# The second part of a 2-D spectral filter: 64x64 fp32 products on quarters of the TensorE array instead of split 128x128 products

## The chip, the cores and the metric

The kernel runs on one core of a Trainium2 chip. A core has a matrix engine (TensorE, PE in the profile), a vector engine (VectorE, DVE), a scalar engine for functions such as exp (ScalarE, ACT), GpSimd (POOL) and a synchronising engine that issues transfers (SP). TensorE reads its operands from SBUF and writes its results to PSUM, which has eight banks of 128 partitions x 2 KB. One bank holds one 128x512 fp32 result. The metric is the device time of one execution, in microseconds (us); the number of a kernel is the median over its runs.

## What is computed

Two independent results stand side by side in the output. The first is multi-query attention: 16 heads share one key and one value of width 28. The second is a global filter: a real 2-D FFT of a 2048 x 448 array, a product with a complex weight for each frequency, and the inverse FFT.

```python
# A: x (1, 2048, 448), 16 heads of 28, one k and one v
q = (x @ wq) as (1, 16, 2048, 28);  k = x @ wk;  v = x @ wv
scores = einsum("bhqd,bkd->bhqk", q, k) * 28 ** -0.5
a = (softmax(scores) @ v, heads side by side) @ wo
# B: x (1, 2048, 448), w_r and w_i (2048, 225)
X = rfft2(x) * (w_r + 1j * w_i)
b = irfft2(X, s=(2048, 448))
out = concatenate([a, b], axis=-1)
```

## The kernel before

**Attention.** Four heads are packed into one group, and there are four groups (g) for each of four chunks of 512 queries (c). Each of these 16 pairs (c, g) has 16 steps, one for each block of 128 keys. A step makes four score tiles of 128x512 (L914, one matmul each, the operands split so that single-pass fp32r products keep fp32 accuracy), takes their exponentials (L846 straight from PSUM on ScalarE), and multiplies them by the values (L857: four fp32 matmuls of 128 rows x 32 columns that run side by side in the four column strips of the array; an fp32 matmul is two passes, so the trace shows eight records). The sums of the 16 steps gather in one PSUM bank.

**Rounds.** Steps are done in rounds. In a round of six steps all 24 score tiles are made first, then the value products of six steps. Some tiles are "lazy": VectorE copies the scores to SBUF (L920) and ScalarE takes their exponentials later, during the value products (L939 or L943). The table `PLAN` lists the rounds as strings: `-` is a score tile whose exponential is taken at once, `k` a lazy tile, `e` a tile of a late step whose exponential ScalarE takes from PSUM (L925), and capital letters are units of other work put between the score tiles. The program itself is written out in that order; each engine executes its own instructions strictly in it.

**Banks.** A score tile or a unit takes a bank with `take()`, and the reader of the result gives it back with `give()`. Which bank is taken is fixed when the program is built, from a model of when each will be free (`clock`, `passed`, `at_once`). One bank holds the running sums of the value products, so seven banks rotate among score tiles and units. VectorE work that can wait is put into a queue (`put`), from which the planner lets it out where its model has VectorE idle; `need` forces it out before an instruction that depends on it.

**The filter.** It has three parts. The first (`fft1`) ends at about 73 us, before the rounds start in earnest. The third (`fft3`, letter Z) has its first matmul at 308.8 us and runs almost to the end. The second part is the one that changes. It works on 16 slices u of two columns each (2 x 225 = 450 frequencies), all 128 partitions. A forward unit (letter A, `fft2_a`) multiplies the slice by a fixed 128x128 matrix g1 (32-point transforms, real and imaginary parts), then VectorE multiplies by the complex weights. A backward unit (letter B, `fft2_b`) multiplies by g2, VectorE copies the result to SBUF (L636), and every second unit a transfer takes it to the DRAM array t2. Both matrix products go through `mm3`: matrix and data are split into a high and a low fp32r half, and three 128x128 products are added up (L567, L568, L569). The splits of the data cost VectorE a cast and a subtraction before each product (L598 and L599 for the forward one, L621 and L622 for the backward one). The complex product is L612 and L613 (each 64 partitions, crossing the halves), L614, and later L620.

The second part lies in 17 rounds between 86.0 and 302.7 us: one round with A alone, eleven with B and A, four with B, A and X (X is four W units, the 11 matmuls of the output projection of one block, L767), and a round of five steps with B alone.

Of the kernel before, what the change touches and what calls it, by code (L numbers as in the profile page):

```python
# [48 lines left out]
PLAN += [spread(6, "A", 6, 1.6, 0.85, 1.5)] + 11 * [spread(6, "BA", 6, 0.9, 0.6, 1.5)]  # L49
PLAN += 4 * [spread(6, "BAX", 5, 0.9, 0.85, 1.5)] + [spread(5, "B")] + [spread(7, "ZZ", 8, 0.9, 0.85, 2.0)]  # L50
# [16 lines left out]
def kernel(ctx: ExitStack, tc: tile.TileContext, t: dict):  # L67
# [120 lines left out]
    def fft2_consts():  # L188
        for n in ("g1", "g2"):
            g = fp.tile([128, 128], F32, name=n, tag="g", bufs=1)  # L190
            nc.gpsimd.dma_start(g, t[n])
            h = fc[n + "h"] = fp.tile([128, 128], F32R, name=n + "h", bufs=1)
            l = fc[n + "l"] = fp.tile([128, 128], F32R, name=n + "l", bufs=1)
            nc.gpsimd.tensor_copy(h, g)
            nc.gpsimd.tensor_tensor(l, g, h.bitcast(F32), op=ALU.subtract)
# [370 lines left out]
    def mm3(out, w, h, l):  # L566
        mm(out, fc[w + "h"], h, start=True, stop=False)  # L567
        mm(out, fc[w + "l"], h, start=False, stop=False)  # L568
        mm(out, fc[w + "h"], l, start=False, stop=True)  # L569
# [5 lines left out]
    def fft2_load(q):  # L575
        b = b2["b", q] = fp.tile([128, 4, DF], F32R, name="b2", tag="b2")
        for r in range(2):
            for l in range(2):
                p = (r * 2 + l) * 32
                ld = nc.sync.dma_start(b[p:p + 32].bitcast(F32), t1v[r, l][:, 4 * q:4 * q + 4])  # L580
# [12 lines left out]
    def fft2_split(u):  # L593
        q, v = divmod(u, 2)
        b = b2["b", q][:, 2 * v:2 * v + 2]
        bh = b2["h", u] = fp.tile([128, 2, DF], F32R, name="bh", bufs=1)
        put(("split", u), [
            (400, lambda: nc.vector.tensor_copy(bh, b.bitcast(F32))),  # L598
            (630, lambda: nc.vector.tensor_tensor(b, b.bitcast(F32), bh.bitcast(F32), op=ALU.subtract))], True)  # L599

    def fft2_a(u):
        q, v = divmod(u, 2)
        s = slice(2 * v, 2 * v + 2)
        b, wr, wi = (b2[n, q][:, s] for n in ("b", "wr", "wi"))
        need(("split", u))
        need(("pr", u - 1))
        bank = take()
        pu = halves2(bank)
        mm3(pu, "g1", b2["h", u], b)
        passed(608)  # L610
        pf, p2 = fp.tile([128, 2, DF], F32, name="pwr"), fp.tile([128, 2, DF], F32, name="pwi")
        nc.vector.tensor_tensor(p2[0:64], pu[64:128], wi[64:128], op=ALU.mult)  # L612
        nc.vector.tensor_tensor(p2[64:128], pu[0:64], wi[0:64], op=ALU.mult)  # L613
        nc.vector.tensor_tensor(pf, pu, wr, op=ALU.mult)  # L614
        at_once(1800)
        give(bank)
        h = fp.tile([128, 2, DF], F32R, name="ph")
        p = fp.tile([128, 2, DF], F32R, name="pl")
        put(("pr", u), [
            (700, lambda: nc.vector.scalar_tensor_tensor(pf, p2, sgn, pf, op0=ALU.mult, op1=ALU.add)),  # L620
            (420, lambda: nc.vector.tensor_copy(h, pf)),  # L621
            (640, lambda: nc.vector.tensor_tensor(p, pf, h.bitcast(F32), op=ALU.subtract))], True)  # L622
        if u < 15:
            fft2_split(u + 1)
        pr[u] = h, p

    def fft2_b(u):
        v = u % 2
        need(("pr", u))
        bank = take()  # L630
        pc = halves2(bank)
        mm3(pc, "g2", *pr.pop(u))
        passed(608)
        if v == 0:
            cst[0] = fp.tile([128, 4, DF], F32, name="cst")
        nc.vector.tensor_copy(cst[0][:, 2 * v:2 * v + 2], pc)  # L636
        at_once(600)
        give(bank)
        if v:
            nc.sync.dma_start(t2[:, 2 * u - 2:2 * u + 2], cst[0])  # L640


    def fft3_consts():
        c = fp.tile([113, 4, 113], F32, name="cs3", tag="wi")
        behind(nc.gpsimd.dma_start(c, t["cs3"]), begun[-1])
        h = fc["cs3h"] = fp.tile([113, 4, 113], F32R, name="cs3h", tag="cs", bufs=1)
        l = fc["cs3l"] = fp.tile([113, 4, 113], F32R, name="cs3l", tag="bh", bufs=1)
# [3 lines left out]
    t2v = t2.rearrange("(r l n) h f -> r l h n f", r=2, l=2)  # L651
    c2 = {}

    def fft3_load(q):
        c2["c", q] = fp.tile([128, 4, DF], F32, name="c2", tag="b2")
        for r in range(2):
            for l in range(2):
                p = (r * 2 + l) * 32

                eng = nc.gpsimd if q == 0 and r else nc.sync  # L660
                eng.dma_start(c2["c", q][p:p + 32], t2v[r, l][:, 4 * q:4 * q + 4])
# [136 lines left out]
    def at(step, f, *a):  # L798
# [3 lines left out]
            "A": [(fft2_a, u) for u in range(16)],  # L802
            "B": [(fft2_b, u) for u in range(16)],
# [14 lines left out]
    at(where["A"][0] - 1, fft2_split, 0)  # L818
    at(where["B"][-1] + 1, fft3_consts)
    for u, step in enumerate(where["A"]):  # L820
        if u % 2 == 0 and u < 14:
            at(step - 1, fft2_load, u // 2 + 1)
    for g in range(2 * NG - 1):
        at(where["B"][g + 1] - 4, wo_load, g)
        at(where["B"][g + 1] + 4, wo_split, g)
    for q in range(8):
        at(max(where["Z"][4 * q] - 8, where["Z"][4 * q - 5] + 1 if q > 1 else where["B"][-1] + 1), fft3_load, q)
# [42 lines left out]
    def after(step):  # L870
# [5 lines left out]
        if step == where["B"][-1] + 1:  # L876
            spans.extend(fp.tile([128, 2, CW], F32, name="p", tag="wr") for _ in range(2))
# [190 lines left out]
def _constants():  # L1068
# [13 lines left out]
    c["sgn"] = np.where(np.arange(128) < 64, -1.0, 1.0)[:, None]  # L1082
# [29 lines left out]
    def blocks(sign):  # L1112
        a, b = np.cos(sign * a32), np.sin(sign * a32)
        e = np.eye(2)
        return np.block([[np.kron(e, a), np.kron(e, b)], [-np.kron(e, b), np.kron(e, a)]])
# [5 lines left out]
def _layout(A_x, A_wq, A_wk, A_wv, A_wo, B_x, B_w_r, B_w_i):  # L1121
# [24 lines left out]
    for n, w in (("wr", B_w_r), ("wi", B_w_i)):  # L1146
        z[n] = np.asarray(w)[:, order].reshape(32, 32, 2, DF).transpose(2, 0, 1, 3).reshape(64, 32, DF)
# [36 lines left out]
```

## Time and profile before

| What | Value |
|---|---|
| median of 3 runs | 636.54 us (636.4 to 636.67) |
| the profiled execution | 636.34 us, of which the span is 634.6 us |
| TensorE busy (its ends are modelled) | 628.0 us, 99% |
| ScalarE busy | 547.4 us, 86% |
| VectorE busy | 450.7 us, 71% |
| GpSimd busy | 61.0 us, 10% |
| granted TensorE clock | 1.0 (full) throughout |

The span runs from the first to the last instruction of the program. A busy TensorE row does not mean that TensorE works at its peak: records of matmuls overlap and their ends are modelled. More is told by the distance from one matmul's start to the next one's, and by the idle time that the profile prints behind a weight load (PEld) with the instruction that ended it. In timelines the columns are the start, the length, the engine, the line, the operation, output and inputs, the shape, and how many equal instructions were merged into the row.

### The profile page before, as it was taken

The numbers are of one execution on the slowest core, as the hardware profiler recorded it, in microseconds if no ns is written. First come the engines' busy times: TensorE is split into PE (matmuls) and PEld (weight loads), VectorE is DVE, ScalarE is ACT, GpSimd is POOL, SyncE is SP. The second block draws the span as 40 slices with busy tenths as digits, with TensorE's granted clock in tenths as the row PEclk, the third lists the DMA queues.
The fourth block names the chain that finished last, engine by engine and source line by source line (L and its number), as shares of the span: only waits on it lengthen the run. The fifth ranks groups of instructions, "written<-read, shape, count | busy, mean of one in ns | idle before, by whom it ended". The sixth has DMA issues, their size and how long they took to land. (4 is left out here: it accounts for less than half of the span.)

```text
span 634.6 us, 12172 instructions
## 1 busy us (share of the span) xinstructions
PE 628.0 (99%) x4442; PEld 378.3 (60%) x4442; DVE 450.7 (71%) x808; ACT 547.4 (86%) x987; POOL 61.0 (10%) x118
## 2 busy tenths in 40 slices
PE   8999999999999999999999999999999999999997
PEld 6877655665565466664555665565556565555555
DVE  5999648989998977676766755277777764467653
ACT  5554999999999998888989998999989989989991
POOL 3021401010321020000110100001010100000000
PEclk9999999999999999999999999999999999999999
DMA  8755972645543734133342403034322322030011
GB/s 272 274 156 159 264 186 52 164 122 143 160 96 98 184 80 123 58 81 129 101 101 56 115 15 82 15 84 145 79 68 76 89 82 74 16 82 14 17 31 61
DMA packets 37315, 66.74 MB, mean 105 GB/s; under 512 B 7945, under 2 KB 21786, under 8 KB 36284
## 3 DMA queue, kind: packets, MB, share of 16 engines
q1 hardware_dynamic: 32032, 52.50, 29.9%
q0 software_dynamic: 4640, 12.48, 7.4%
q8 instruction: 36, 0.59, 0.4%
q10 hardware_dynamic: 576, 0.92, 0.4%
q14 instruction: 31, 0.25, 0.1%
HBM read 29.81 MB, written 17.87 MB: 75 GB/s over the span
## 5 line engine op out<-in xcount | busy, mean ns | idle before, releaser
L846 ACT ACTIVATE p<-s 128x512 f32<-128x512 f32 x425 | 234.7, 645 | 25.0 <-PE s L914 24.5
L914 PE MATMUL s<-qa,ka 128*128 128x512 f32 x779 | 235.0, 404 | 0.0
L914 PEld LDWEIGHTS s<-qa,ka 128*128 128x128 f32 x779 | 142.1, 188 | 63.6 <-issue 27.7
L920 DVE COPY k<-s 128x512 f32<-128x512 f32 x116 | 77.0, 687 | 87.4 <-PE s L914 87.1
L857 PE MATMUL s<-p,vs 128*32 128x512 f32 x936 | 129.0, 594 | 0.0
L939 ACT ACTIVATE k<-k 128x1024 f32<-128x1024 f32 x76 | 79.4, 1146 | 0.0
L846 ACT ACTIVATE qraw<-s 128x512 f32<-128x512 f32 x107 | 61.3, 633 | 11.9 <-PE s L914 11.8
L857 PEld LDWEIGHTS s<-p,vs 128*32 128x32 f32 x936 | 32.9, 110 | 63.1 <-issue 57.0
L914 PE MATMUL sx<-qa,ka 128*128 128x512 f32 x127 | 51.0, 402 | 0.0
L914 PE MATMUL po<-qa,ka 128*128 128x512 f32 x118 | 47.8, 405 | 0.0
L857 PE MATMUL s<-qraw,vs 128*32 128x512 f32 x208 | 46.8, 595 | 0.0
L846 ACT ACTIVATE p<-sx 128x512 f32<-128x512 f32 x68 | 44.3, 652 | 1.3 <-PE sx L914 1.3
L846 ACT ACTIVATE p<-po 128x512 f32<-128x512 f32 x65 | 42.0, 646 | 2.3 <-PE po L914 2.3
L920 DVE COPY p<-s 128x512 f32<-128x512 f32 x61 | 40.6, 683 | 0.5 <-PE s L914 0.4
L731 POOL DMA_DIRECT2D ol<-ol x36 | 18.0, 508 | 213.4 <-DVE ol L754 108.8
L857 PE MATMUL po<-p,vs 128*32 128x512 f32 x272 | 36.7, 595 | 0.0
L857 PE MATMUL s<-k,vs 128*32 128x512 f32 x264 | 34.5, 594 | 0.0
L914 PEld LDWEIGHTS sx<-qa,ka 128*128 128x128 f32 x127 | 23.9, 188 | 9.2 <-issue 3.4
L914 PEld LDWEIGHTS po<-qa,ka 128*128 128x128 f32 x118 | 22.2, 188 | 9.6 <-issue 2.5
L939 ACT ACTIVATE p<-p 128x1024 f32<-128x1024 f32 x24 | 26.1, 1140 | 0.0
L857 PE MATMUL sx<-p,vs 128*32 128x512 f32 x148 | 23.9, 595 | 0.0
L352 PE MATMUL s<-xh,wqh 128*128 128x512 f32 x56 | 22.7, 406 | 1.0 <-ACT wqh L332 1.0
(295 smaller groups left out, 994.2 us busy)
## 6 DMA issues: line engine op xcount, KB each, us to landing
qa<-qa SPq DMA_DIRECT2D x15, 512.0 KB
raw<-xa SPq DMA_DIRECT2D x16, 256.0 KB
xb<-xb SPq DMA_DIRECT2D x8, 512.0 KB
qa<-qh SPq DMA_DIRECT2D x64, 64.0 KB
qa<-ql SPq DMA_DIRECT2D x60, 64.0 KB
t<-bs SPq DMA_DIRECT2D x16, 225.0 KB
wr<-wr POOLq DMA_DIRECT2D x16, 225.0 KB, 3.9
wi<-wi POOLq DMA_DIRECT2D x16, 225.0 KB, 5.5
```

The source lines that it names most:

```text
L352: mm(pq, w[:, j, gs], x[:, j], start=(j == 0 and n == 0), stop=(j == 3 and n == 1))
L731: nc.gpsimd.dma_start(ol[c][o, g].bitcast(F32), ol[c][r, 0].bitcast(F32))
L846: nc.scalar.activation(tiles[-1][:, h % 2], sc, AF.Exp, scale=SCALE)
L857: mm(po[c, g][32 * i:32 * i + 32], vs[:, kc], ps[i // 2][:, i % 2], start=(n == 1), stop=(n == 16))
L914: begun.append(mm(sc, ka[:, kc * 128:(kc + 1) * 128], qa[c, g][:, h], start=True, stop=True))
L920: nc.vector.tensor_copy(keep[i][h // 2][:, h % 2], sc)
L939: nc.scalar.activation(p, p, AF.Exp, scale=SCALE)
```

## The change

The matrices are no longer 128x128. In the 128x128 matrix g1 half of the entries are zero, because two interleaved 32-point transforms share it; sorted by transform it is two 64x64 blocks on the diagonal. After the change the partitions are sorted that way (the loads of t1 and t2, `sgn`, `wr` and `wi` follow), g1 and g2 are 128x64 arrays that hold the block twice, and each product is two unsplit fp32 matmuls of 64 rows x 64 columns, one on each half of the partitions (`quarters`). The forward product uses the upper left and the lower right quarter of the array; the backward product, with `turn=1`, uses the other two and leaves its halves exchanged, which the loads of part three undo.

One unit Q (`fft2(u)`) does the forward product of slice u and the backward product of slice u - 1, right behind each other in the program, so that all four quarters have work. It needs two banks at once. There are 17 of them: the first has no backward half and the last no forward half. The splits fall away. The crossing product now goes in four pieces of 32 partitions (L615 after) instead of two of 64. The weights arrive with one transfer each instead of two.

```diff
-PLAN += [spread(6, "A", 6, 1.6, 0.85, 1.5)] + 11 * [spread(6, "BA", 6, 0.9, 0.6, 1.5)]
-PLAN += 4 * [spread(6, "BAX", 5, 0.9, 0.85, 1.5)] + [spread(5, "B")] + [spread(7, "ZZ", 8, 0.9, 0.85, 2.0)]
+PLAN += [spread(6, "Q", 6, 1.6, 0.85, 1.5)] + 11 * [spread(6, "Q", 6, 0.9, 0.6, 1.5)]
+PLAN += 4 * [spread(6, "QX", 5, 0.9, 0.85, 1.5)] + [spread(5, "Q")] + [spread(7, "ZZ", 8, 0.9, 0.85, 2.0)]
...
-    def mm3(out, w, h, l):
-        mm(out, fc[w + "h"], h, start=True, stop=False)
-        mm(out, fc[w + "l"], h, start=False, stop=False)
-        mm(out, fc[w + "h"], l, start=False, stop=True)
+    def quarters(out, w, x, turn):
+
+        for l in range(2):
+            o, r = 64 * (l ^ turn), slice(64 * l, 64 * l + 64)
+            mm(out[o:o + 64], fc[w][r], x[r], start=True, stop=True)
...
-        for n in ("wr", "wi"):
-            b2[n, q] = fp.tile([128, 4, DF], F32, name=n)
-            for r in range(2):
-                ld = nc.gpsimd.dma_start(b2[n, q][64 * r:64 * r + 64], t[n][:, 4 * q:4 * q + 4])
-                behind(ld, begun[-1])
+            behind(nc.gpsimd.dma_start(b2[n, q], t[n][:, 4 * q:4 * q + 4]), begun[-1])
...
-    def fft2_split(u):
...
-    def fft2_a(u):
...
-    def fft2_b(u):
...
+    def fft2(u):
+
+        if u:
+            need(("pr", u - 1))
+            pc = take()
+        if u < 16:
+            q, v = divmod(u, 2)
+            b, wr, wi = (b2[n, q][:, 2 * v:2 * v + 2] for n in ("b", "wr", "wi"))
+            pu = take()
+            quarters(halves2(pu), "g1", b, 0)
+        if u:
+            quarters(halves2(pc), "g2", pr.pop(u - 1), 1)
+        passed(950)
+        if u:
+            v = (u - 1) % 2
+            if v == 0:
+                cst[0] = fp.tile([128, 4, DF], F32, name="cst")
+            nc.vector.tensor_copy(cst[0][:, 2 * v:2 * v + 2], halves2(pc))
+            at_once(600)
+            give(pc)
+            if v:
+                nc.sync.dma_start(t2[:, 2 * u - 4:2 * u], cst[0])
+        if u < 16:
+            x = halves2(pu)
+            pf, p2 = fp.tile([128, 2, DF], F32, name="pwr"), fp.tile([128, 2, DF], F32, name="pwi")
+            for p in range(0, 128, 32):
+                i, o = slice(p, p + 32), slice(p ^ 32, (p ^ 32) + 32)
+                nc.vector.tensor_tensor(p2[o], x[i], wi[i], op=ALU.mult)
+            nc.vector.tensor_tensor(pf, x, wr, op=ALU.mult)
+            at_once(2900)
+            give(pu)
+            put(("pr", u), [(700, lambda: nc.vector.scalar_tensor_tensor(pf, p2, sgn, pf, op0=ALU.mult, op1=ALU.add))],
+                True)
+            pr[u] = pf
```

With the new rules each of the eleven rounds reads `-k--k-k--k-k--kQ-------ee` instead of `-k--k-k--kB-k--k---A----ee`: one interruption behind 15 score tiles instead of two behind 10 and 18. Each of the four rounds with X reads `-k--k-k-Q-k-k----WWWW-----eee` instead of `-k--k-Bk--k-k-A----WWWW----eee`.

The first place is TensorE in the second of the eleven rounds (the one that starts at 110.74 us in the trace of before), from the tile ahead of unit A to the first value product. The name ahead of the arrow is the bank; qa and ka are the queries and keys of the score tiles.

```order
L914 MATMUL s4_89<-qa_1131,ka_67 128x512
L567 MATMUL s3_88<-bh_1387,g1h_1067 128x450
L568 MATMUL s3_88<-bh_1387,g1l_1068 128x450
L569 MATMUL s3_88<-b2_1261,g1h_1067 128x450
L914 MATMUL sx_1116<-qa_1131,ka_67 128x512
L914 MATMUL s1_86<-qa_1131,ka_67 128x512
L914 MATMUL s0_85<-qa_1131,ka_67 128x512
L914 MATMUL po_1117<-qa_1131,ka_67 128x512
L914 MATMUL s5_90<-qa_1131,ka_67 128x512
L914 MATMUL s4_89<-qa_1131,ka_67 128x512
L857 MATMUL s2_87<-p10_1061,vs_68 32x512 x2
```

The last score tile (s4) reuses the bank of the tile ahead of A, which is the twelfth `-` tile of the round. Now the same stretch of the changed kernel, from the tile ahead of unit Q (its line of the score matmul is L893).

```order
L893 MATMUL s3_88<-qa_1121,ka_67 128x512
L566 MATMUL sx_1108<-b2_1250,g1_1065 64x450 x2
L566 MATMUL s4_89<-pwr_1350,g2_1067 64x450 x2
L893 MATMUL s5_90<-qa_1121,ka_67 128x512
L893 MATMUL s2_87<-qa_1121,ka_67 128x512
L893 MATMUL po_1109<-qa_1121,ka_67 128x512
L893 MATMUL s0_85<-qa_1121,ka_67 128x512
L893 MATMUL s3_88<-qa_1121,ka_67 128x512
L893 MATMUL s4_89<-qa_1121,ka_67 128x512
L893 MATMUL s5_90<-qa_1121,ka_67 128x512
L893 MATMUL s2_87<-qa_1121,ka_67 128x512
L893 MATMUL po_1109<-qa_1121,ka_67 128x512
```

Nine tiles instead of six follow the unit, and the last one again reuses the bank of the twelfth `-` tile (po), which now stands behind the unit and not ahead of it.

The second place is TensorE earlier in the same round of the changed kernel, tiles 6 to 12 of 24.

```order
L893 MATMUL po_1109<-qa_1121,ka_67 128x512
L893 MATMUL s3_88<-qa_1121,ka_67 128x512
L893 MATMUL s0_85<-qa_1121,ka_67 128x512
L893 MATMUL s4_89<-qa_1121,ka_67 128x512
L893 MATMUL sx_1108<-qa_1121,ka_67 128x512
L893 MATMUL s5_90<-qa_1121,ka_67 128x512
L893 MATMUL po_1109<-qa_1121,ka_67 128x512
```

Tile 12 is given the bank of tile 6, the fourth `-` tile. It is so in four of the eleven rounds (the second, fifth, seventh and tenth); in the other seven tile 12 gets the bank of the second `k` tile.

The third place is VectorE in the first of the rounds with X, before the change: `k` copies (L920), the copy out of a backward unit (cst, L636), the complex product (L612 to L614, L620), and the copy of an output block (ya).

```order
L920 COPY k<-sx 128x512
L920 COPY k<-s_88 128x512
L218 TENSOR_TENSOR ql<-ql,qh 128x512
L636 COPY cst<-s_86 128x450
L920 COPY k<-s_85 128x512
L920 COPY k<-po 128x512
L920 COPY p_1056<-s_89 128x512
L612 TENSOR_TENSOR pwi<-s_86,wi 64x450
L613 TENSOR_TENSOR pwi<-s_86,wi 64x450
L614 TENSOR_TENSOR pwr<-s_86,wr 128x450
```

After the change the same round reads:

```order
L899 COPY k<-s_89 128x512
L899 COPY k<-s_86 128x512
L899 COPY k<-po 128x512
L214 TENSOR_TENSOR ql<-ql,qh 128x512
L605 COPY cst<-s_89 128x450
L615 TENSOR_TENSOR pwi<-sx,wi 32x450 x4
L616 TENSOR_TENSOR pwr<-sx,wr 128x450
L899 COPY k<-s_86 128x512
L899 COPY p_1056<-po 128x512
L756 COPY ya<-s_88 128x448
```

The last two copies of lazy tiles now stand behind the six instructions of the unit. From the round that follows the last unit on, the order of TensorE and its use of banks are the same in both kernels but for the banks' names.

More of the change, by code (lines that the diff above doesn't have):

```diff
@@ L591, in halves2 @@
         return bank[:, :2 * DF].rearrange("p (n f) -> p n f", n=2)
-    def fft2_split(u):
[L594 to L599, printed above, removed]
-    def fft2_a(u):
[L602 to L625, printed above, removed]
@@ L817 @@
     at(1, fft2_load, 0)
-    at(where["A"][0] - 1, fft2_split, 0)
-    at(where["B"][-1] + 1, fft3_consts)
-    for u, step in enumerate(where["A"]):
+    at(where["Q"][-1] + 1, fft3_consts)
+    for u, step in enumerate(where["Q"]):
         if u % 2 == 0 and u < 14:
```

52 lines of the change are left out of this document (17 added, 35 removed).

## The prediction

> **What bounds the kernel now.** I read the page first, then TensorE's timeline over whole rounds, then ScalarE and the weight loads (PEld) of one round.
>
> ```profile
> PE 628.0 (99%) x4442; PEld 378.3 (60%) x4442; DVE 450.7 (71%) x808; ACT 547.4 (86%) x987; POOL 61.0 (10%) x118
> ```
>
> The page alone says TensorE. The rounds that hold the second part say more. The next rows are first score matmuls of rounds: the round with A alone (86.01 to 98.39), eleven rounds with B and A (98.39 to 234.62), four with X (to 292.65), and the last (to 302.69).
>
> ```profile
> 86.01 0.73 PE L914 MATMUL s<-qa,ka 128*128 128x512 f32 x2
> ...
> 93.10 0.64 PE L857 MATMUL s<-p,vs 128*32 128x512 f32 x4
> ...
> 98.39 0.73 PE L914 MATMUL s<-qa,ka 128*128 128x512 f32 x2
> ...
> 234.62 0.50 PE L914 MATMUL s<-qa,ka 128*128 128x512 f32 x1
> ...
> 292.65 0.50 PE L914 MATMUL po<-qa,ka 128*128 128x512 f32 x1
> ...
> 302.69 0.72 PE L914 MATMUL s<-qa,ka 128*128 128x512 f32 x2
> ```
>
> The eleven rounds take (234.62 - 98.39) / 11 = 12.38 us each. But the round before them, which has only one unit, takes the same 12.38. If TensorE alone set the pace it would be one unit shorter. So something else holds these rounds at 12.38. One of the eleven shows it:
>
> ```profile
> 110.74 0.73 PE L914 MATMUL s<-qa,ka 128*128 128x512 f32 x2
> ...
> 112.91 0.39 PE L914 MATMUL s<-qa,ka 128*128 128x512 f32 x1
> 113.14 0.36 PE L567 MATMUL s<-ph,g2h 128*128 128x450 f32 x1
> ...
> 113.75 0.40 PE L914 MATMUL s<-qa,ka 128*128 128x512 f32 x1
> ...
> 115.61 0.37 PE L567 MATMUL s<-bh,g1h 128*128 128x450 f32 x1
> ...
> 116.22 0.39 PE L914 MATMUL sx<-qa,ka 128*128 128x512 f32 x1
> ...
> 117.81 1.06 PE L857 MATMUL s<-p,vs 128*32 128x512 f32 x8
> ...
> 123.10 0.50 PE L914 MATMUL sx<-qa,ka 128*128 128x512 f32 x1
> ```
>
> ```profile
> 111.34 0.60 ACT L846 ACTIVATE p<-s 128x512 f32<-128x512 f32 x1 [0.54 <-PE s L914]
> ...
> 116.17 1.15 ACT L846 ACTIVATE p<-s 128x512 f32<-128x512 f32 x2
> 117.13 0.69 ACT L846 ACTIVATE p<-sx 128x512 f32<-128x512 f32 x1
> ...
> 117.38 0.19 PEld L914 LDWEIGHTS s<-qa,ka 128*128 128x128 f32 x1 [0.26 <-ACT p L846]
> ```
>
> ScalarE starts 0.60 after the round's first score and then runs without a gap: its 13th exponential stands at 117.13, so one comes every (117.13 - 111.34) / 12 = 0.48. The 12th ends at 116.17 + 1.15 = 117.32. At 117.38 the weight load of the last score tile begins, after 0.26 of waiting for ScalarE: it needs the bank that the 12th exponential frees (front, first order). Then come the value products, 117.81, and 5.29 later the next round, 123.10. So a round is a chain: first score, 0.60, twelve exponentials back to back, last score, value products. TensorE is close behind (the 0.26 of that wait is all it has to spare), but the chain ends last, and ScalarE never starves in it, because B and A interrupt the scores for only 113.75 - 113.14 = 0.61 and 116.22 - 115.61 = 0.61. In the A round the value products also start at 7.09 (93.10 - 86.01) against 7.07 here.
>
> **What a unit Q costs TensorE.** The trace has fp32 products of 64x64 blocks in part one (L169), there 225 columns wide:
>
> ```profile
> 59.80 0.41 PE L169 MATMUL pbb<-a,fw 64*64 64x225 f32 x2
> ...
> 60.05 0.36 PE L169 MATMUL pbb<-a,fw 64*64 64x225 f32 x2
> ...
> 60.24 0.36 PE L169 MATMUL pbb<-a,fw 64*64 64x225 f32 x2
> ...
> 60.43 0.36 PE L169 MATMUL pbb<-a,fw 64*64 64x225 f32 x2
> 60.44 0.36 PE L169 MATMUL po<-a,fw 64*64 64x225 f32 x2
> 60.73 0.50 PE L352 MATMUL s<-xh,wqh 128*128 128x512 f32 x1
> 61.06 0.39 PE L352 MATMUL s<-xl,wqh 128*128 128x512 f32 x1
> ```
>
> Four quarters run one pass together in 0.19 (60.24 to 60.43), two passes make the product; the first pass takes 0.25. With 450 columns, twice as many, I estimate 0.38 a pass, so 0.76 and 0.06 for the first. Changing the shape costs more. Leaving it: 60.73 - 60.44 = 0.29 instead of 0.19, and the next interval is 0.33 where score matmuls go at 0.23 (112.91 to 113.14): 0.10 twice. Entering it is priced by the change from scores to 32-column value products, where no bank is waited for:
>
> ```profile
> 243.36 0.63 PE L914 MATMUL s<-qa,ka 128*128 128x512 f32 x2
> 243.91 0.64 PE L857 MATMUL po<-p,vs 128*32 128x512 f32 x4
> ```
>
> The second score starts 0.23 after 243.36, the products 0.32 after that: 0.09 too much. From below the entry is free, from above it costs 0.2 (117.81 in the round above: 0.66 after the pair at 117.15, two tenths over two intervals, with a bank wait in it); I take 0.09, the same kind of change without a wait. So from the score ahead of Q to the one behind it pass 0.32 + 0.44 + 0.38 + 0.10 = 1.24, and 0.10 more in the interval after: Q adds 1.24 - 0.23 + 0.10 = 1.11. A pair B and A added 2 x 0.61 = 1.22. The half-empty first and last Q cost the same 1.11, since a pass is as long with two quarters. By TensorE's sum alone: 17 x 1.11 - 32 x 0.61 = 18.9 - 19.5 = -0.6 us. Little is saved there.
>
> **What the eleven rounds become.** Clock from the first score. Fifteen scores come first, the 15th at 0.33 + 13 x 0.23 = 3.32; Q follows, and the 16th score starts at 4.56. Its exponential starts 0.60 later, as behind the change of shape at the round's start (110.74 to 111.34), at 5.16. Nine tiles went to ScalarE ahead of Q; it is through with them at 0.60 + 9 x 0.48 = 4.92. So ScalarE idles 0.24. The last score again needs the bank of the 12th exponential, which is now behind Q, and all of the 0.24 arrives in the value products. In four rounds tile 12 waits for the fourth exponential (front, second place): it ends at 0.60 + 3 x 0.48 + 0.62 (0.60 to 0.69 in the rows), and with the 0.06 of 117.32 to 117.38 the load starts at 2.72 and takes 0.19, while TensorE would start the tile at 0.33 + 10 x 0.23 = 2.63. That is up to 0.28 late; I take 0.18, since the load of 117.38, 0.26 late, held the products up by less than that. So 0.42 in these four. Sum: 7 x 0.24 + 4 x 0.42 = **+3.4 us**. From below 0 (the chain can't get shorter: twelve exponentials keep their 0.48), from above 6 with 0.2 for each entry.
>
> **The other rounds.** First Q: 14 of the `-` tiles stand ahead of it, and by the 20th score, 0.33 + 18 x 0.23 = 4.47, ScalarE has begun only nine, so it doesn't starve and the round stays at its 12.38: 0 (up to 0.5). Last Q: eight tiles ahead, TensorE sets the pace: 1.11 - 0.61 = 0.5, less what the round waits already; **+0.4**. The four with X:
>
> ```profile
> 237.45 0.60 ACT L846 ACTIVATE p<-sx 128x512 f32<-128x512 f32 x1 [0.16 <-PE sx L914]
> ...
> 242.63 2.06 ACT L846 ACTIVATE p<-s 128x512 f32<-128x512 f32 x4 [1.08 <-PE s L914]
> ```
>
> Here ScalarE has room (1.08 idle at X), and the value products start at 243.91 - 234.62 = 9.29. Q comes behind eight tiles, five of them `-`: next score 0.33 + 6 x 0.23 + 1.24 = 2.95, its exponential 3.55, ScalarE free at 0.60 + 5 x 0.48 = 3.00: 0.55 idle against 0.16 at B before. Two lazy copies now stand behind Q's six VectorE instructions (front, third place; 0.63 each, rows below) and hold their banks to about 8. So the eight scores behind Q find few banks: W, due at 2.95 + 0.33 + 7 x 0.23 = 4.89, takes the bank of the eighth exponential, which ends at 3.55 + 2 x 0.48 + 0.62 = 5.13, some 0.25 late, and the last score is some 0.15 late for the thirteenth exponential, now behind W. Against the 0.11 that TensorE saves I estimate 0.35 each, **+1.4 us** (from -0.1 by TensorE's sum to +0.6).
>
> **VectorE and the queues.**
>
> ```profile
> L612 DVE TENSOR_TENSOR pwi<-s,wi 64x450 f32<-64x450 f32 x12 | 7.5, 628 | 2.1 <-PE s L569 1.3 <-ACT p L846 0.5
> L614 DVE TENSOR_TENSOR pwr<-s,wr 128x450 f32<-128x450 f32 x12 | 7.5, 627 | 0.3
> ...
> L599 DVE TENSOR_TENSOR b<-b,bh 128x450 fp32r<-128x450 f32 x16 | 10.1, 628 | 0.5
> L622 DVE TENSOR_TENSOR pl<-pwr,ph 128x450 fp32r<-128x450 f32 x16 | 9.9, 621 | 0.4
> L598 DVE CAST bh<-b 128x450 fp32r<-128x450 f32 x16 | 6.2, 387 | 0.0
> L621 DVE CAST ph<-pwr 128x450 fp32r<-128x450 f32 x16 | 6.3, 396 | 0.5
> ```
>
> Four splits leave, (628 + 621 + 387 + 396) ns = 2.03 a slice. Two products of 32 partitions come in; 64 and 128 partitions take the same 0.63, so 32 do too (half would be the lower end): 1.26. VectorE gains 0.77 a slice, 12 us in all, worth nothing: the chain names ScalarE, not VectorE. What does change is that the forward bank is held through five products behind one copy, 4.5 + 6 x 0.63 = 8.3 after the round's start, past the last score; in the eleven rounds unit A's bank was held past it too, so the count of banks is unchanged. The t1 loads and t2 stores on SP stay as many; GpSimd issues two weight transfers instead of four per load, and is 10% busy. Part three keeps its order, 0.
>
> Sum: 3.4 + 0 + 1.4 + 0.4 = +5.2. The profiled 636.34 (a span of 634.6 and 1.7 around it) becomes 641.5; it stands 0.2 below the median, so I predict **641.7 us**, 0.8% slower. Own range 638.2 to 645.5.
>
> **Rivals.**
> - TensorE's sum holds: banks free early enough, so that ScalarE's idle time is caught up. For it: ScalarE has 0.54 idle at a round's start (row 111.34). Against: that time lies in front of the first score, not where the 12th exponential is due. -0.6: 635.9.
> - The other side, faster: the changes of shape overlap with the neighbouring scores, so that Q costs its 0.76 alone. Place: the 16th score. It would start at 3.32 + 0.23 + 0.76 = 4.31, its exponential at 4.9, when ScalarE is free, 4.92. Then the eleven rounds stay at 12.38, X rounds gain 1.22 - 0.76 = 0.46 each, the last loses 0.15: 634.8. It decides as soon as Q adds less than about 0.8. Against: every change in these rows is paid.
> - The quarters don't run together. In L169 the two row halves write different banks (pbb and po); in Q both halves of the forward product write one bank. No row shows that. If they take turns, Q lasts 0.76 longer, all of it on the chain: 641.7 + 17 x 0.76 = 654.6. Against: they write different partitions. The Trainium skill ("TensorEngine Tiling (Array Packing)", Gotcha 1: PSUM Pressure) says that different row tiles cannot access the same PSUM bank at once, which would give this time; its page "PSUM — Partial Sum Buffer" (PSUM bank collisions raise a hardware error) narrows the harm to one bank and the same 32 partitions, which Q avoids. No run here shows either yet.
>
> **Chances.** My forecast 0.72; TensorE's sum 0.11; faster 0.08; quarters in turn 0.05; in the remaining 0.04 the X rounds or later waits take it to 646 to 650. Anything within 0.2% (1.3 us) is about what a measurement can't tell from no change. Faster 0.08; within 0.2%: 0.12, the TensorE sum and the edge of my case; slower 0.80. A range of 636.6 to 646 leaves out the faster case, about half of the second, the quarters in turn and the rest: 0.2.
>
> **What would show it.** After: L566 matmuls in fours at 0.38 a pass, 1.24 around Q; rounds of 12.6 to 12.8, with a ScalarE gap of 0.25 to 0.45 behind Q that names L893; X rounds up by 0.3; nothing changed after 308. Wrong would make it: no ScalarE gap behind Q; a last score tile that no longer waits for ScalarE; passes of 0.76.

## The result, and the profile after

The changed kernel takes **643.24 us** (median of 4 runs, 641.98 to 644.07), the kernel before 636.47 us beside it (635.61 to 636.67): a ratio of 1.0107, with a 95% interval of 1.0088 to 1.0126. It is 1.1% slower; 641.7 was predicted. The profiled execution took 643.28 us, with a span of 641.5.

The busy shares alone tell little: TensorE 99% as before, VectorE 69% instead of 71%. The first score matmuls of the rounds tell where the time went. TensorE's timeline of the kernel after (the score matmul is L893 now):

```profile
98.37 0.51 PE L893 MATMUL s<-qa,ka 128*128 128x512 f32 x1
...
110.87 0.51 PE L893 MATMUL s<-qa,ka 128*128 128x512 f32 x1
...
236.72 0.50 PE L893 MATMUL s<-qa,ka 128*128 128x512 f32 x1
...
295.68 0.50 PE L893 MATMUL sx<-qa,ka 128*128 128x512 f32 x1
...
306.02 0.50 PE L893 MATMUL po<-qa,ka 128*128 128x512 f32 x1
...
324.67 0.50 PE L893 MATMUL sx<-qa,ka 128*128 128x512 f32 x1
```

In before the same rounds begin at 98.39, 110.74, 234.62, 292.65, 302.69 and 317.91. The differences of neighbours are the stages:

| Stage | before | after | difference | forecast |
|---|---|---|---|---|
| all up to the first Q's end | 98.39 | 98.37 | 0.0 | 0 |
| eleven rounds | 136.23 | 138.35 | +2.1 | +3.4 |
| four X rounds | 58.03 | 58.96 | +0.9 | +1.4 |
| last Q round | 10.04 | 10.34 | +0.3 | +0.4 |
| the round behind it (first of part three) | 15.22 | 18.65 | **+3.4** | 0 |
| the rest of the span | 316.6 | 316.8 | +0.2 | 0 |

So the stages with Q cost 3.3 us, less than the forecast 5.2, and a round in which nothing had been changed cost as much again.

**Q itself.** The third of the eleven rounds, from the score ahead of Q to the score behind it:

```profile
126.90 0.39 PE L893 MATMUL s<-qa,ka 128*128 128x512 f32 x1
127.25 0.59 PE L566 MATMUL s<-b,g 64*64 64x450 f32 x2
127.27 0.59 PE L566 MATMUL s<-pwr,g 64*64 64x450 f32 x2
127.68 0.54 PE L566 MATMUL s<-b,g 64*64 64x450 f32 x2
127.70 0.54 PE L566 MATMUL s<-pwr,g 64*64 64x450 f32 x2
128.17 0.51 PE L893 MATMUL sx<-qa,ka 128*128 128x512 f32 x1
```

All four quarters begin within 0.02 us of each other, and the second pass starts 0.43 after the first. In this round Q waits a little for a bank. Where it doesn't (the X rounds), 0.33 pass from the score ahead to the first pass, 0.43 to the second and 0.49 from there to the next score: 1.24 before rounding, the value that was forecast.

**What ScalarE does.** The second of the eleven rounds, one of the four whose tile 12 waits for the fourth exponential:

```profile
111.47 1.58 ACT L825 ACTIVATE p<-s 128x512 f32<-128x512 f32 x3 [0.53 <-PE s L893]
112.92 0.62 ACT L825 ACTIVATE p<-po 128x512 f32<-128x512 f32 x1
113.40 2.59 ACT L825 ACTIVATE p<-s 128x512 f32<-128x512 f32 x5
116.20 1.09 ACT L825 ACTIVATE p<-s 128x512 f32<-128x512 f32 x2 [0.21 <-PE s L893]
117.17 0.60 ACT L825 ACTIVATE p<-po 128x512 f32<-128x512 f32 x1
```

Nine exponentials stand ahead of Q. The ninth starts at 113.40 + 4 x 0.48 = 115.3, the tenth at 116.20: 0.90 instead of 0.48, a gap of 0.42, and what ended it is the score behind Q. The profile prints only 0.21 of idle time, because exponentials overlap: one is 0.6 to 0.7 long, and one starts every 0.48. The forecast for this kind of round was 0.42. In five of the other seven the gap is 0.24 to 0.25 (forecast 0.24). The fourth and the eighth have 0.34: there the second row half of the forward product starts 0.10 behind the first instead of 0.01, for which the profile gives no reason. The twelfth exponential starts 5.70 after the first (117.17 - 111.47), where it was 5.31 before ((117.13 - 111.34) x 11 / 12), so 0.39 of the gap arrive there. But it is only 0.60 long, where the twelfth of before took 0.67 (it ended at 117.32). The value products come 0.31 later, not 0.42.

**The round that nobody touched.** TensorE behind the last Q round, after:

```profile
307.96 0.40 PE L893 MATMUL sx<-qa,ka 128*128 128x512 f32 x1
310.61 1.10 PE L652 MATMUL s<-fi,c 128*113 128x128 f32 x8 [2.25 <-DMA c<-t]
...
313.06 0.63 PE L893 MATMUL s<-qa,ka 128*128 128x512 f32 x1
313.48 0.63 PE L893 MATMUL sx<-qa,ka 128*128 128x512 f32 x1
```

and the same wait before:

```profile
305.29 1.10 PE L671 MATMUL po<-fi,c 128*113 128x128 f32 x8 [0.26 <-DMA c<-t]
```

The first product of part three waits 2.25 us for its data c, 2.0 more than before. And then scores run 0.43 apart instead of 0.23. The reason for that stands in a view of stretches of time (busy time of each engine, then the granted TensorE clock, the DMA share and GB/s):

```profile
core 0: us, PE busy (x) PEld busy (x) DVE busy (x) ACT busy (x) POOL busy (x), PEclk, DMA share, GB/s
...
312.50:314.20 1.70, 1.70 (x5) 1.31 (x5) 1.67 (x4) 1.25 (x4) 0.00 (x0) 0.50 0.00 1
```

The clock was granted at half behind the wait, from 311.8 to 315.2 us; eight intervals of 0.43 instead of 0.23 are another 1.6 us. This does not happen in every run: the run of 641.98 us has a mean of 1.0, the other three 0.995 to 0.997.

**Why c is late.** SP's own queue, before and then after. qd<-qraw is the store of a slice of q (1 MB), t<-cst the last store of part two, c<-t the loads of part three that need it:

```profile
286.94 0.59 SPq L881 DMA_DIRECT2D qd<-qraw  x1
297.16 0.33 SPq L640 DMA_DIRECT2D t<-cst  x1
298.27 2.55 SPq L728 DMA_DIRECT2D oh<-ol  x4
300.93 0.85 SPq L661 DMA_DIRECT2D c<-t  x2
```

```profile
293.10 5.21 SPq L709 DMA_DIRECT2D oh<-ol  x8
298.35 0.60 SPq L860 DMA_DIRECT2D qd<-qraw  x1
300.38 0.33 SPq L609 DMA_DIRECT2D t<-cst  x1
306.07 2.72 SPq L642 DMA_DIRECT2D c<-t  x6
```

The eight small transfers oh<-ol belong to two normalisations on VectorE. Relieved of the splits, VectorE ends these ahead of the last Q round instead of in it:

```profile
297.50 0.69 DVE L754 TENSOR_TENSOR ol<-osb,oh 128x512 fp32r<-128x512 f32 x1
...
300.32 0.69 DVE L754 TENSOR_TENSOR ol<-osb,oh 128x512 fp32r<-128x512 f32 x1
```

```profile
292.33 0.69 DVE L735 TENSOR_TENSOR ol<-osb,oh 128x512 fp32r<-128x512 f32 x1
...
295.15 0.69 DVE L735 TENSOR_TENSOR ol<-osb,oh 128x512 fp32r<-128x512 f32 x1
```

So the small transfers now stand ahead of the 1 MB store on SP. The store waits behind them, and is issued 2 us ahead of t<-cst instead of 10. (That the missing splits moved the normalisations is read from this order; no run tests it alone.) From the issue of t<-cst to the first load of c pass 5.69 us instead of 3.77. That the late store is the cause is the first theory to be tested; the second is that the rounds with Q are longer because ScalarE runs dry behind one long interruption. The rivals: the change of the array's shape costs TensorE the time; the banks that Q holds cost it; the late loads come from the later last unit.

### The profile page after: what moved, and what is told of

It reads as the page before. It is cut to its first block, busy times and chain, and to the rows that moved or that the text cites. A ratio compares the mean times of both kernels' runs of the same rounds, so it can differ in the third digit from the quotient of the medians.

```text
span 641.5 us, 12122 instructions
## 1 busy us (share of the span) xinstructions
PE 633.1 (99%) x4474; PEld 362.7 (57%) x4474; DVE 440.6 (69%) x776; ACT 548.6 (86%) x987; POOL 51.0 (8%) x98
## 5 line engine op out<-in xcount | busy, mean ns | idle before, releaser
L825 ACT ACTIVATE p<-s 128x512 f32<-128x512 f32 x394 | 221.2, 639 | 23.4 <-PE s L893 22.1
L893 PE MATMUL s<-qa,ka 128*128 128x512 f32 x733 | 231.1, 409 | 0.0
L836 PE MATMUL s<-p,vs 128*32 128x512 f32 x1356 | 188.9, 594 | 0.0
L893 PEld LDWEIGHTS s<-qa,ka 128*128 128x128 f32 x733 | 133.6, 189 | 72.0 <-issue 22.6
L836 PEld LDWEIGHTS s<-p,vs 128*32 128x32 f32 x1356 | 47.5, 110 | 92.1 <-issue 85.3
L836 PE MATMUL s<-qraw,vs 128*32 128x512 f32 x348 | 74.3, 595 | 0.0
L825 ACT ACTIVATE p<-sx 128x512 f32<-128x512 f32 x86 | 55.2, 642 | 6.5 <-PE sx L893 6.5
L893 PE MATMUL po<-qa,ka 128*128 128x512 f32 x148 | 60.3, 407 | 0.0
L893 PE MATMUL sx<-qa,ka 128*128 128x512 f32 x143 | 58.5, 409 | 0.0
L836 PE MATMUL s<-k,vs 128*32 128x512 f32 x344 | 44.9, 593 | 0.0
L840 DVE STREAM_TRANSPOSE osb<-s 128x512 f32<-128x512 f32 x16 | 11.4, 716 | 35.4 <-PE s L836 35.3
L893 PEld LDWEIGHTS po<-qa,ka 128*128 128x128 f32 x148 | 28.1, 190 | 13.5 <-issue 4.2
L893 PEld LDWEIGHTS sx<-qa,ka 128*128 128x128 f32 x143 | 27.0, 189 | 15.2 <-issue 5.9
L836 PEld LDWEIGHTS s<-qraw,vs 128*32 128x32 f32 x348 | 16.7, 110 | 23.3 <-issue 21.1
L899 DVE COPY k<-po 128x512 f32<-128x512 f32 x25 | 17.2, 688 | 12.1 <-PE po L893 12.1
```

What stands on the lines that cost most here:

```text
L825: nc.scalar.activation(tiles[-1][:, h % 2], sc, AF.Exp, scale=SCALE)
L836: mm(po[c, g][32 * i:32 * i + 32], vs[:, kc], ps[i // 2][:, i % 2], start=(n == 1), stop=(n == 16))
L840: nc.vector.transpose(o, po[c, g])
L893: begun.append(mm(sc, ka[:, kc * 128:(kc + 1) * 128], qa[c, g][:, h], start=True, stop=True))
L899: nc.vector.tensor_copy(keep[i][h // 2][:, h % 2], sc)
```

## The experiments

**1. The 1 MB store ahead of the small transfers.** In the kernel after, one line:

```diff
-        if c < NC - 1 and g == 40:
+        if c < NC - 1 and g == (38 if c == 1 else 40):
```

> The kernel after, with one transfer moved: the 1 MB store qd<-qraw of the second slice is issued two steps earlier, ahead of the eight oh<-ol transfers on SP's queue; nothing else changes place on any engine. If the store is what slows the last t2 store, and with it the first loads of part three, the round after the last Q round falls from 18.65 to about 15.3 us, its wait for c from 2.25 to about 0.3, and the time from 643.2 to about 639.9. If the later VectorE work, the eight oh<-ol transfers or the later last unit itself delay the loads, that round stays above 18 and the time at 643.

Measured: 639.97 us, 1.0054 of before (1.0041 to 1.0068). The round goes from 18.65 to 14.77 and its wait for c is gone. SP's queue in this kernel:

```profile
284.30 0.59 SPq L860 DMA_DIRECT2D qd<-qraw  x1
...
293.72 5.21 SPq L709 DMA_DIRECT2D oh<-ol  x8
301.00 0.33 SPq L609 DMA_DIRECT2D t<-cst  x1
303.93 2.71 SPq L642 DMA_DIRECT2D c<-t  x6
```

The small transfers stand where they stood, and the loads come 2.93 behind t<-cst instead of 5.69. The view of transfers from 297 to 312 us, in 40 slices, shows how: the busy share of the 16 DMA engines in tenths and GB/s, after and then here.

```profile
DMA  0111110924899999999999100017895999988997
GB/s 22 28 28 27 28 33 11 224 62 155 349 400 393 382 393 388 393 426 439 392 422 384 67 0 0 0 26 202 178 351 166 389 226 199 273 176 253 326 278 127
```

```profile
DMA  0001120149588599700007897999999998320000
GB/s 11 5 16 39 22 44 6 44 101 193 185 285 350 227 403 413 307 10 0 0 0 158 221 295 171 312 336 228 204 243 245 246 276 154 50 58 5 0 0 0
```

After, the engines are full from 301 to 305 us at 380 to 440 GB/s: the store (1.0 MB), t<-cst (450 KB) and two loads on GpSimd's queue (cs and fi, 200 and 256 KB) use them, 1.9 MB in all. By the trace's records of single packets t<-cst comes last: its last packet moves at 305.67, 5.29 us behind its issue, and the loads that wait for it start 0.40 later. Here the store is not among them, and t<-cst is through 2.55 us behind its issue. The store's 1.0 MB at 390 GB/s are 2.6 us, and the gain between t<-cst and the loads is 2.76. So without the store's traffic the loss is gone, with the later unit and the small transfers where they were.

**2. The same from the other side, in before.** First by placing the store one step later:

```diff
-        if c < NC - 1 and g == 40:
+        if c < NC - 1 and g == (41 if c == 1 else 40):
```

> The kernel before, with the same store held back to one step later, so that it is issued about 2 us ahead of the last t2 store, as in the kernel after; no order on any queue or engine changes. If the store next to the t2 store is the cause, the c loads start 2 to 2.6 us later than their 300.3, the round behind goes from 15.22 to 17 or 18.6, and the time from 636.5 to 638.5 to 639.9. If the cause lies in something else that the change moved, the time stays at 636.5.

Measured: 638.49 us, 1.0032 (1.0016 to 1.0049). The edit did not do what it was meant to: the store was still issued at 287.07, since nothing made SP wait, and the planner put two small ol<-ol transfers ahead of the c loads on GpSimd's queue instead. So the time answers another question: GpSimd's two c loads were issued at 302.92 and 303.50 instead of 300.34 and 300.90, and the round grew to 16.98. With GpSimd's c loads 2.6 us late this round is 1.8 longer, from a cause that is not the store. In the eighth experiment the store really waits:

```diff
-            behind(nc.sync.dma_start(qd[...], qraw[...]), begun[-1])
+            st = nc.sync.dma_start(qd[...], qraw[...])
+            if c == 1:
+                tc.add_manual_dep(st.ins, begun[-1].ins.name,
+                                  mybir.DependencyInfo(mybir.DependencyClass.Sync, mybir.DependencyReason.DATA),
+                                  reason="late store")
```

> The kernel of the second experiment (before, with two ol<-ol transfers ahead of the c loads on GpSimd's queue), in which the store now really comes late: it waits on SP for the twelfth score matmul of the last B round, about 2.5 us into it, so that it is issued some 2 us ahead of the last t2 store. If the 1 MB store slows the t2 store, the time from that store's issue to the first c load on SP grows from 3.8 us to about 6, the c loads come some 2 us later, the round behind grows from 16.98 to 18 or 19, and the time is 638.5 plus 1 to 2. If the store is harmless and only the oh<-ol transfers ahead of it or the later unit mattered in the kernel after, the c loads start 3.8 us behind the t2 store as before and the time stays at 638.5.

Measured: 637.87 us, 1.0028 (1.0019 to 1.0038), and the round 16.90: no longer than in its control. SP's queue:

```profile
294.57 0.59 SPq L881 DMA_DIRECT2D qd<-qraw  x1
295.84 0.33 SPq L640 DMA_DIRECT2D t<-cst  x1
...
300.23 0.86 SPq L661 DMA_DIRECT2D c<-t  x2
```

The loads come 4.39 behind t<-cst instead of 3.77, only 0.6 later, and the round did not grow. That does not clear the store. By the packet records the last packet of t<-cst moves 4.01 us behind its issue, against 2.10 in the second experiment, so the store alone holds t<-cst up by 1.9 us (it is issued 1.27 us ahead of t<-cst here, 2.03 in after). Two things hide it. On SP four oh<-ol transfers stand between t<-cst and the loads, so that the loads started 1.67 us behind the last packet in the second experiment and start 0.38 behind it here; in after nothing stands between. And this kernel, like its control, has GpSimd's c loads late (301.47 and 302.06, behind SP's), so SP's loads could move without moving the round. So the first experiment shows that taking the store away removes the loss, and the packets of this one show the store's delay of t<-cst without the loads cs and fi. How much of after's 5.29 is due to cs and fi was not tested by moving them alone.

**3. Q later in the eleven rounds.**

```diff
-11 * [spread(6, "Q", 6, 0.9, 0.6, 1.5)]
+11 * [spread(6, "Q", 6, 1.6, 0.85, 1.5)]
```

> The kernel after, with Q in the eleven rounds behind the 20th score, where the first Q stands, instead of behind the 15th. If those rounds are longer because ScalarE runs out of scores behind Q (0.25 and 0.42 us of gap), there is no gap any more, the rounds return from 12.50 to 12.68 to about 12.37, and the time falls by 2.1 to about 641.1. If they are longer because Q costs TensorE more than B and A did, or because Q holds two banks through seven VectorE instructions, they stay at 12.5 to 12.7 or grow, and the time is 643 or more.

Measured: 645.1 us, 1.0142 (1.0126 to 1.0157), slower than after. The gaps of ScalarE are gone, as the theory said, and yet seven rounds take 12.79 to 12.85 and four 12.59 to 12.66. The weight loads of the first of them, with their waits, show why:

```profile
103.48 0.14 PEld L566 LDWEIGHTS s<-b,g 64*64 64x64 f32 x2 [0.30 <-ACT p L825]
...
105.44 0.19 PEld L893 LDWEIGHTS s<-qa,ka 128*128 128x128 f32 x1 [0.30 <-ACT p L825]
```

Q now waits for a bank from ScalarE, and so does the last score. In the program's order the last score of the seven long rounds has the bank of the 13th exponential, not of the 12th: one exponential more in the chain, 0.48, and 12.37 + 0.48 = 12.85. (By its times the 13th exponential ends about 7.1 us into the first of these rounds, and the last score starts at 7.13.) In the four others it has the bank of Q's own backward half. The forecast of 12.37 had counted ScalarE's supply and not the banks: Q late takes two banks that the last scores need. The theory of the dry ScalarE is not refuted by this, but it was only half of the account.

**4. In before, A and B directly behind each other at Q's place.** No 64x64 blocks, the same products:

```diff
-11 * [spread(6, "BA", 6, 0.9, 0.6, 1.5)]
+11 * [spread(6, "BA", 6, 90, 158, 1.5)]
```

> The kernel before, with its units B and A directly behind each other, at the place that Q has in the kernel after (behind the 15th score), in the eleven rounds; same products, full array, no 64x64 blocks. If the length of one interruption starves ScalarE, the pair (1.22 in one piece, against 1.01 of Q) leaves it idle for about 0.45 to 0.6, and the rounds go from 12.37 to 12.7 to 12.9: +4 to +5, time about 641. If it is the change of the array's shape that costs, the rounds stay at 12.37 and the time at 636.5.

Measured: 638.49 us, 1.0039 (1.0024 to 1.0054). The eleven rounds take 138.96 instead of 136.23 (first scores at 97.78 and 236.74). ScalarE in the first of them:

```profile
101.73 1.16 ACT L846 ACTIVATE p<-s 128x512 f32<-128x512 f32 x2
103.02 0.60 ACT L846 ACTIVATE p<-sx 128x512 f32<-128x512 f32 x1
```

From the ninth exponential (101.73 + 0.48 = 102.21) to the tenth pass 0.81: a gap of 0.33, where after had 0.25. So full-array products do to ScalarE what Q does, once they stand in one piece, and somewhat more: from the score ahead of them to the score behind them they add 1.23 us, Q adds 1.01. Changes of shape are not needed for the loss; they count only as a part of Q's length. The size was again smaller than expected (0.2 a round, 0.41 to 0.48 in three, instead of 0.3 to 0.5).

**5. Half of each product of Q.** On the kernel of the first experiment; the other half of the columns of the filter's second part is left out:

```diff
-            mm(out[o:o + 64], fc[w][r], x[r], start=True, stop=True)
+            mm(out[o:o + 64, :1], fc[w][r], x[r][:, :1], start=True, stop=True)
```

> The kernel of the first experiment (after, with the early store), with every product of Q made over the first 225 of its 450 columns only; the other half of the filter's second part is left out, VectorE's work and the banks stay. Both passes of Q get shorter, together by about 0.43 us. If the length of the interruption is what starves ScalarE, its gaps of 0.25 and 0.42 behind Q vanish, the eleven rounds return to about 12.37 (2.1 us in all), the X rounds to about 14.5 and the last Q round to about 10.0, and the time goes from 640.0 to about 637.0. If the two banks that Q holds through seven VectorE instructions make the rounds longer, the rounds stay at 12.50 to 12.68 and the time at 640.

Measured: 635.51 us, 0.9990 of before (0.9980 to 0.9999). The eleven rounds:

```profile
98.45 0.50 PE L893 MATMUL s<-qa,ka 128*128 128x512 f32 x1
...
234.32 0.50 PE L893 MATMUL s<-qa,ka 128*128 128x512 f32 x1
```

That is 12.35 each, with the banks held and VectorE's work as in after. ScalarE in the second of them (in after the row breaks off there, and the tenth exponential starts at 116.20):

```profile
113.32 3.57 ACT L825 ACTIVATE p<-s 128x512 f32<-128x512 f32 x7
```

Seven exponentials follow each other across Q. In the eleven rounds no gap behind Q is over 0.03; X rounds take 14.37, the last Q round 10.00. All three stages go back to where they were or below. With the length of Q the cost goes away, so the banks held through VectorE's seven instructions do not make it.

**6 and 7. Seven lazy tiles, after and before.** The chain through the twelfth exponential can be shortened by one, if VectorE copies one tile more:

```diff
-11 * [spread(6, "Q", 6, 0.9, 0.6, 1.5)]
+11 * [spread(6, "Q", 7, 1.0, 0.6, 1.5)]
```

> The kernel of the first experiment, with seven instead of six score tiles of each of the eleven rounds copied out by VectorE (one more copy of 0.63 us a round, paid from the 0.77 a round that the change freed there), Q behind the 17th score; so the last score takes the bank of the 11th exponential instead of the 12th. If the chain over ScalarE sets these rounds, they lose most of one exponential, 0.48, until ScalarE's own sum stops them (24 exponentials of 0.48 and 0.54 idle ahead of them make 12.1): 12.1 to 12.3 each, 2 to 6 us in all, and the time goes from 640.0 to 634 to 638. If VectorE can't carry the copy or TensorE sets the pace, the rounds stay at 12.5 or grow.

```diff
-11 * [spread(6, "BA", 6, 0.9, 0.6, 1.5)]
+11 * [spread(6, "BA", 7, 0.9, 0.6, 1.5)]
```

> The kernel before, with the same seventh copy in the eleven rounds. Here VectorE has the four splits of each unit pair to do as well (2.03 us a round). If the time that the change frees on VectorE is what pays for the seventh copy, these rounds get longer here (VectorE's sum of a round goes from about 12 to over 12.4), and the time is 637 to 642. If a seventh copy would do as well without the change, the rounds fall to 12.1 to 12.3 and the time to 632 to 635.

Measured: the sixth 635.19 us, 0.9988 (0.9978 to 0.9997); the seventh 635.24, 0.9984 (0.9975 to 0.9993). The rounds of the sixth and then of the seventh:

```profile
97.76 0.50 PE L893 MATMUL s<-qa,ka 128*128 128x512 f32 x1
...
232.27 0.51 PE L893 MATMUL s<-qa,ka 128*128 128x512 f32 x1
```

```profile
98.36 0.50 PE L914 MATMUL s<-qa,ka 128*128 128x512 f32 x1
...
233.34 0.51 PE L914 MATMUL s<-qa,ka 128*128 128x512 f32 x1
```

12.23 and 12.27 a round. The chain did set the rounds: one exponential less brings the changed kernel 0.35 a round (12.58 in experiment 1) of the 0.48. Then TensorE takes over: of the scores behind Q none after the first waits for ScalarE any more (in after the last two did), though ScalarE still has its gap of 0.25 (0.43 in two rounds). But the expectation for before was wrong: VectorE carries the seventh copy there too (127.2 of 135.0 us busy between 98.36 and 233.34). What the change frees on VectorE is not needed for this.

**9. Q later in the X rounds,** on the kernel of the sixth:

```diff
-4 * [spread(6, "QX", 5, 0.9, 0.85, 1.5)]
+4 * [spread(6, "QX", 5, 1.2, 1.2, 1.5)]
```

> The kernel with seven copies, with Q in the four X rounds behind ten tiles instead of eight (six exponentials ahead of it instead of five), and X still behind sixteen tiles. If X comes late there because it waits for the bank of the eighth exponential, which stands behind Q, then X now needs that of the seventh and starts at 4.9 instead of 5.1 us, and the last score, which needs the bank of the second exponential behind X, follows: 0.2 us a round, 14.74 to about 14.53, and the time from 635.2 to about 634.3. If the X rounds are longer because of what Q costs TensorE, they stay at 14.74.

Measured: **633.80 us**, 0.9972 of before (0.9961 to 0.9983), the fastest of all, and faster than before and after. The X rounds fall from 14.74 to 14.42, where 14.53 was expected. X's first weight load, in an X round of after and then here (that round starts at 246.67):

```profile
256.59 0.19 PEld L748 LDWEIGHTS s<-woh,oh 128*128 128x128 f32 x1 [0.30 <-ACT p L825]
```

```profile
251.35 0.19 PEld L748 LDWEIGHTS s<-woh,oh 128*128 128x128 f32 x1
```

X started 5.13 into its round (that one at 251.46) with a wait for ScalarE, and starts 4.68 into it without one.

## Why the prediction came out as it did

The total was close, 641.7 against 643.24. But its parts were not: three errors of size, 1.9 us together, to one side, and an omission of 3.4 to the other. That they nearly cancel is luck.

- **The eleven rounds, +3.4 forecast, +2.1 measured.** The mechanism holds. The gaps were 0.25 and 0.42 as worked out, they vanish with half of Q (experiment 5), and they come without 64x64 blocks when B and A stand together (experiment 4). The term mis-sized is "all of the 0.24 arrives in the value products": of 0.25 arrive 0.14, of 0.42 some 0.31. About 0.07 is given back because the twelfth exponential behind a gap is 0.60 long and not 0.67, and 0.04 because before had a break of that length behind B (its twelfth exponential started 5.31 behind the first; without any break it is 5.27). Eight of the rounds fall short of the forecast by 0.09 to 0.14 each. The tenth falls short by 0.39, mostly because it took 12.63 in before already, with a gap of 0.33 behind B that the forecast's mean of 12.38 hid. The fourth and the eighth, with their 0.34, came out as forecast.
- **The first Q, 0.** Measured 12.36 against 12.38. The reason given was supply of ScalarE; experiment 3 shows that it also needs a bank to spare, which only this half-empty unit leaves.
- **The X rounds, +1.4 forecast, +0.9 measured.** The place was right: X began 5.13 into the round, as worked out, and waited for ScalarE, and so did the last score; with Q later, X no longer waits (experiment 9). The delay was 0.23 and not 0.35 a round. The forecast's own terms, 0.25 and 0.15 less 0.11, make 0.29.
- **The last Q round,** +0.4 forecast, +0.3 measured.
- **Q on TensorE.** 1.24 from score to score, as forecast, though a pass takes 0.43 and not 0.38 and the way out less. A half-empty Q has the same pass of 0.43 (91.06 to 91.49 in after). That TensorE alone would gain 0.6 agrees with what is left once the other waits are shorter, though it is no proof of it: from experiment 7 to experiment 9 the eleven rounds, the four with X and the last go from 134.98, 58.06 and 10.04 to 134.52, 57.67 and 10.33, together -0.56.
- **The quarters in turn** did not happen. In Q the two row halves of the forward product write one bank, on different partitions, and start 0.01 us apart (0.10 in the fourth and the eighth round), within a pass of 0.43. The Trainium skill ("TensorEngine Tiling (Array Packing)", Gotcha 1: PSUM Pressure) says that different row tiles cannot access one PSUM bank at the same time; the trace shows two doing so, and the narrower statement of "PSUM — Partial Sum Buffer" (PSUM bank collisions raise a hardware error), one bank and the same 32 partitions, fits it.
- **The failed step: "The t1 loads and t2 stores on SP stay as many", "Part three keeps its order, 0" and "nothing changed after 308".** The number of transfers stayed; their order did not. The time that VectorE gained (12 us by the forecast, 10.1 by the pages: 450.7 to 440.6) was called worth nothing, and its price was not asked: earlier VectorE work issues its transfers earlier, and behind these the 1 MB store ran into the last store of part two. Experiment 1 takes 3.3 us back with one line, and in its profile the whole round is 0.45 below before's. Of the 3.4, 2.0 are the longer wait and about 1.6 the half clock behind it, less 0.2 won elsewhere in the round. In experiment 3 this round has nearly the same wait (2.12) at full clock and takes 17.10, which puts the half clock at some 1.4.
- **A sum in the rivals.** For the case "faster", 636.54 less 1.84 and 0.15 is 634.55, not 634.8; nothing else hangs on it.

TensorE's order from that round on was the same in both kernels, and the forecast took this for the whole answer. The order of SP's queue would have shown the eight transfers ahead of the store before anything ran.

## What to carry to other kernels

Two short interruptions of a stream that feeds another engine can be free where one of the same total length is not: count how many tiles the fed engine has in hand at that place, with the banks that the unit itself takes, and not only the array's time. And when an engine is relieved, ask what it will do earlier: compare the order of every queue that it feeds, down to the first transfer on which the next stage waits. After such a change the tables of order want to be set anew: with four numbers of the plan and the place of one store changed, the same unit Q went from 1.1% slower than before to 0.3% faster. Most of that is not Q's own merit: the kernel before, with one number of its plan changed, is 0.2% faster too (experiment 7).

## What the runs showed of the hardware

- Behind an idle time of 2.25 us TensorE ran for 3.4 us (311.8 to 315.2) at a granted clock of 0.50. Waits of 1.93, 2.01 and 2.1 us at the same place in experiments 8, 2 and 3 were followed by full clock. One run of after has a mean of 1.0, so no half clock either; it left no trace. The clock records of the eleven traces suggest why. Within a trace the granted clock changes at times that lie whole multiples of 3.413 us apart (in after at 4.59, 311.79, 315.20 and 639.47). In stretches between such times, half clock followed where TensorE was busy for 1.41 us or less (1.17 and 1.41 in after, 1.36 at the end of experiment 2), and full clock where it was busy for 1.53 or more (1.53 at the end of experiment 5, 1.59 in experiment 3). So what counted was how much of one fixed stretch was idle; the waits of experiments 2, 3 and 8 each fell across the border of two. The Trainium skill ("TensorE: Matmul & The Clock Gate", Part 1: The HAM clock gate) has the clock halved after an idle window of about 3.4 us and restored after about 3.4 us of work. The second figure fits this trace; the first does not as it stands, since 2.25 us of idle time were enough here.
- Four transfers of 1.9 MB together ran at 380 to 440 GB/s with all 16 engines busy, and the 450 KB of t<-cst, issued last, were through last: 5.29 us behind their issue, against 2.55 without the 1 MB store (experiment 1), 4.01 with the store and without the two loads (experiment 8) and 2.10 with neither (experiment 2).
- Exponentials that follow each other are 0.60 long at first and 0.67 by the twelfth in before's rounds, and 0.77 where no gap stands ahead at all (the first Q round), at an unchanged distance of 0.48; after a gap of 0.25 they are at 0.60 again. So a gap in such a row costs less than its length.
